# A linear-attention and gated-FFN kernel: ten gathering copies moved from SyncE's queue to GpSimd's, and per-tile waits for the pool of FFN weights

## The chip, the cores and the metric

The kernel runs on one core of one Trainium2 chip. The metric is the device time of one execution in microseconds (us); lower is better. The engines are TensorE (PE, with its weight loads PEld), VectorE (DVE), ScalarE (ACT), GpSimd (POOL) and SyncE (SP). Each engine works off its own row of instructions in order. Transfers are issued by an instruction on SP, ACT or POOL and then run by themselves.

## The reference

There are S = 2048 tokens of width D = 576, 32 heads of width 18, and an FFN of width F = 4608; all is float32.

```
xn = layernorm(x)
q, k, v = split(xn @ wqkv)                     # 32 heads of 18
pq, pk = q @ w_phi, k @ w_phi                  # a matrix of 18 x 18 for each head
phi_q = [softmax(pq), softmax(-pq)]            # 36 features a head
phi_k = [softmax(pk), softmax(-pk)]
num = phi_q @ (phi_k^T v);  den = phi_q . sum(phi_k) + 1e-6
s = (num / den) @ wo
g = silu((silu(xn @ w_gate) * (xn @ w_up)) @ w_down)
out = x + s * g
```

## The kernel before

Every float32 operand of a product is split into a high part and a rest, both fp32r (`split`, L62 to L64: a cast on ACT, a subtraction on DVE), and a product is three matmuls. The tokens are worked in tiles of 128.

**Stages.** First comes the layernorm. Then in the K/V stage each token tile gives its features `phi` (`k_tile`), and `kv_step` sums `phi^T v` in PSUM (`kvp`). Then the Q stage: for each token tile `q_tile` computes `e` (the softmax parts, L312 to L325), multiplies it with the sums of the keys into `ez` (L627), divides, and writes `e` (L637); `numer` transposes `e` on PE (L656) and multiplies with the numerator's weights; `project` multiplies with `wo` (L697). Last comes the FFN, in which gate and up products (L815) and down products (L936) are done by a scheme of seven products for eight, with sums of weights and operands made on POOL. Matmuls of some early FFN tiles (`early_weights`, `early_tile`, L97 for the matmuls) are put between those of the Q stage. The weights of such a tile are loaded into `raw` (L114, on SP), cast into `wh` (L67, ACT), and completed on DVE (L68, L69).

**The numerator's weights.** Behind the K/V stage `kvp` is masked into `km` (L561) and split. The groups of seven heads go to `KVH` and `KVL`. The last group, of four heads (72 rows), is split into `km2`, which lies in a buffer named `phi` of the pool `kk`. It is packed so that one matmul holds more rows: ten small transfers from SBUF to SBUF (four of 54 x 72 and six of 18 x 72 numbers) gather the parts into `KVP` (108 partitions). PE reads `KVP` at L669, with `et`, a packed copy of the last group of `e` that ACT makes (L641 and L642).

**Sums of the token blocks.** The FFN's scheme needs sums of blocks of tokens. For one block after another, POOL adds them (`raw_x`, `sums`), ACT and POOL split them (`sum_parts`, L364 to L366), and SP stores them to `sum_dram` (L367, L368). The last block is done at the beginning of the Q stage.

**What sets the order.** The engines' rows are set when the kernel is built: a scheduler takes the instructions as they are written, `tc.high_priority` moves some ahead where their inputs allow, and `tc.issue_after` holds some back. Waits between engines are set by the data, and by memory. A pool's tiles may take the place of tiles of a pool that is closed. With `reuse_waits="tile"` a new tile waits for those older tiles whose places it takes; without it the pool's first tile waits for all that lay in the memory that the pool takes over. The pool `fw` of the FFN's weights (L729) has no such argument: its tiles are `ld` (one loaded block of gate and up weights, L763), `ts` (sums of it), `w2` and `w1` (split parts, shown as `w`), and `wt`, which DVE clears once (L734). The Q stage's pool `qk` takes over memory of `kk`: its first `ez` has the place of `km2`.

**The opening of the FFN.** POOL makes four sums from `ld` (L791 to L794), ACT and DVE split `ld` and the sums (L63, L64), PE multiplies into `px`, `py`, `pw` (L815), and ACT copies `px` to `py` (L869) and to `s` (L844). POOL's `td` (L1058) is a sum of down weights that were loaded into `acc` (L1182). On POOL's row the stores of the last early tile (L137) stand between these sums.

Of the kernel before, what the change touches and what calls it, by code (L numbers as in the profile page):

```python
# [9 lines left out]
F32 = mybir.dt.float32  # L10
# [7 lines left out]
S, D, H, DH, F = 2048, 576, 32, 18, 4608  # L18
P = 128
# [10 lines left out]
NL = GROUPS[-1][1]  # L30
NK = NL + NL // 2
N3 = NK // 2
# [10 lines left out]
def heads(ap):  # L43
    return ap.rearrange("p (h d) -> p h d", d=DH)


def spread(ap, n):
    return ap.unsqueeze(2).to_broadcast([P, n, DH])
# [3 lines left out]
def gated_hedgehog_kernel(ctx: ExitStack, tc, x, w_qk, w_v, w_phi, wo, w_gu, w_tail, w_down, ident_in, mask_in, out):  # L52
# [5 lines left out]
    nc = tc.nc  # L58
# [3 lines left out]
    def split(hi, lo, src):  # L62
        nc.scalar.copy(hi, src)  # L63
        nc.vector.tensor_sub(lo, src, hi)  # L64
# [19 lines left out]
    def block(t):  # L84
        return t // HT, (t % HT) // 4, slice((t % 4) * P, (t % 4 + 1) * P)

    def xw(ps, i, j, cols, wh, wl, stationary_x):
        pairs = []
        for k in range(2):
            b = XB[i][2 * j + k]  # L90
            for c in range(2):
                pairs += [(b[:, c, cols], w[:, k, c]) for w in (wh, wl)]
                pairs += [(b[:, 3 + c, cols], wh[:, k, c])]
            pairs += [(b[:, 2, cols], wh[:, k, 2])]
        for n, (a, b) in enumerate(pairs):
            l, r = (a, b) if stationary_x else (b, a)
            last = nc.tensor.matmul(ps, l, r, start=n == 0, stop=n == len(pairs) - 1)  # L97
        return last
# [42 lines left out]
    with ExitStack() as att:  # L141
# [17 lines left out]
        with ExitStack() as wst:  # L159
# [191 lines left out]
            def sums(k):  # L351
                r = raws[k]
                nc.gpsimd.tensor_add(r[:, 3], r[:, 2], r[:, 3])
                nc.gpsimd.tensor_sub(r[:, 2], r[:, 0], r[:, 2])
                nc.gpsimd.tensor_sub(r[:, 0], r[:, 3], r[:, 0])
                nc.gpsimd.tensor_sub(r[:, 1], r[:, 1], r[:, 0])

            def sum_parts(k):
                r = raws[k]
                lo = los[k] = kk.tile([P, 4, 2, P], F32R, name="slo", bufs=1)  # L360
                for a in (2, 0):
                    j = slice(a, a + 2)
                    hi = his[k, a] = kk.tile([P, 2, 3, P], F32R, name="shi", bufs=2)
                    tc.keep_in_program_order(nc.scalar.copy(hi, r[:, j]))  # L364
                    nc.gpsimd.tensor_sub(hi[32:64, :, 2], r[32:64, j, 2], hi[32:64, :, 2])
                    nc.gpsimd.tensor_sub(lo[:, j], r[:, j, 0:2], hi[:, :, 0:2])  # L366
                    nc.sync.dma_start(sum_dram[k // 4, :, j, k % 4, 0:3], hi.bitcast(F32))  # L367
                    nc.sync.dma_start(sum_dram[k // 4, :, j, k % 4, 3:5], lo[:, j].bitcast(F32))  # L368
# [162 lines left out]
        with ExitStack():  # L531
            qc = att.enter_context(tc.tile_pool(name="qc", bufs=1, reuse_waits="tile"))
            KVH = qc.tile([GW, 2 * NG - 2, GW], F32R, name="KVH")
            KVL = qc.tile([GW, 2 * NG - 2, GW], F32R, name="KVL")
            zb = qc.tile([P, 2 * D], F32, name="zb")
            zc = qc.tile([GW, 12], F32, name="zc")
            m4 = mask.rearrange("p h d -> p (h d)")
            km2 = kk.tile([P, 2 * D], F32R, name="phi", bufs=2)[0:NL, 0:4 * NL].rearrange("p (a s n) -> p a s n", a=2, s=2)
            km2 = [km2[:, a] for a in range(2)]
            banks = [(i, 4 if i < 2 else 2, GROUPS[2 * i][1]) for i in range(3)]  # L540
            for i, n, w in banks:
                nc.scalar.copy(zc[0:w, 4 * i:4 * i + n], kvp[i][0:w, 0:n, w])
            z2, oz = zb.rearrange("p (s n) -> p s n", s=2), GROUPS[-1][0]

            def z_rows(d, g, s):
                w = GROUPS[g][1]
                nc.tensor.matmul(d, zc[0:w, 2 * g + s:2 * g + s + 1].to_broadcast([w, P]), ident[0:w, 0:w],
                                 start=True, stop=True)

            for s, name in enumerate(("vx", "vy")):  # L550
                zp = kps.tile([P, 512], F32, name=name)
                for g, (o, w) in enumerate(GROUPS[:-1]):
                    z_rows(zp[:, o:o + w], g, s)
                nc.scalar.copy(z2[:, s, 0:oz], zp[:, 0:oz])
            zp = kps.tile([P, 512], F32, name="vx")
            for s in range(2):
                z_rows(zp[:, s * NL:(s + 1) * NL], NG - 1, s)
            nc.scalar.copy(z2[:, :, oz:D], zp[:, 0:2 * NL].rearrange("p (s n) -> p s n", s=2))
            for i, n, w in banks:
                km = qc.tile([GW, 4, GW], F32, name="km")  # L560
                nc.vector.tensor_mul(km[0:w, 0:n, 0:w], kvp[i][0:w, 0:n, 0:w],  # L561
                                     m4[0:w, 0:w].unsqueeze(1).to_broadcast([w, n, w]))
                kh, kl = (t[0:w, 4 * i:4 * i + n, 0:w] for t in (KVH, KVL)) if n == 4 else km2
                split(kh, kl, km[0:w, 0:n, 0:w])
            KVP = qc.tile([NK, 3, NL], F32R, name="KVP")
            for s in range(2):
                for a, t in enumerate(km2):
                    nc.sync.dma_start(KVP[s * N3:(s + 1) * N3, a].bitcast(F32), t[0:N3, s].bitcast(F32))
                for b, t in enumerate((km2[0], *km2)):
                    r = (2 * b + s) * DH  # L570
                    nc.sync.dma_start(KVP[r:r + DH, 2].bitcast(F32), t[N3:NL, s].bitcast(F32))

        raw_x(order[7], 0, 1)
        raw_x(order[7], 2, 3)
        sums(order[7])
        sum_parts(order[7])
        kst.close()
        eps = est.enter_context(tc.tile_pool(name="eps2", bufs=2, space=PSUM, reuse_waits="tile"))
        with ExitStack() as qst:
# [38 lines left out]
            def q_tile(t):  # L618
                i0, j0, cols = block(t)
                pq = qps.tile([P, 2, 512], F32, name="p2")  # L620
                for i in range(2):
                    w = slice(i * HALF, (i + 1) * HALF)
                    xw(pq[:, i, 0:HALF], i0, j0, cols, QH[:, :, :, w], QL[:, :, :, w], True)
                e = qk.tile([P, 2 * D], F32, name="e", bufs=4)
                r = softmax_parts(pq, e).rearrange("p (s h) -> p s h", s=2)
                ez = qk.tile([P, 2 * D], F32, name="ez", bufs=1)
                nc.vector.tensor_mul(ez, e, zb)  # L627
                y = qk.tile([P, 2 * H], F32, name="y")
                nc.vector.reduce_sum(y, heads(ez), axis=AX.X)
                y2 = y.rearrange("p (s h) -> p s h", s=2)  # L630
                nc.vector.scalar_tensor_tensor(y2[:, 0], r[:, 0], DEN_EPS, y2[:, 0], op0=ALU.mult, op1=ALU.add)
                nc.vector.tensor_mul(y2, y2, r[:, ::-1])
                den = qk.tile([P, H], F32, name="den")
                nc.vector.tensor_add(den, y2[:, 0], y2[:, 1])
                nc.vector.reciprocal(den, den)
                nc.vector.tensor_mul(y2, r[:, ::-1], den.unsqueeze(1).to_broadcast([P, 2, H]))
                last_e.append(nc.vector.tensor_mul(heads(e), heads(e), spread(y, 2 * H)))  # L637
                et = qk.tile([P, 2, NK], F32, name="et", bufs=2)
                o = GROUPS[-1][0]
                e2 = e.rearrange("p (s n) -> p s n", s=2)  # L640
                nc.scalar.copy(et[:, 0].rearrange("p (s n) -> p s n", s=2), e2[:, :, o:o + N3])  # L641
                nc.scalar.copy(et[:, 1].rearrange("p (b s n) -> p b s n", b=3, s=2),  # L642
                               e2[:, :, o + N3:D].unsqueeze(1).to_broadcast([P, 3, 2, DH]))
                return e, et

            def numer(es):
# [61 lines left out]
            for n in range(S // QS + 1):  # L708
                new = []
                if n > 0:  # L710
                    om = numer(es)
                if n < S // QS:
                    new += [q_tile(order[n] * (QS // P) + j) for j in range(QS // P)]
                if n == 0:
                    split_wo()
                if n > 0:
                    project(order[n - 1], *om, n == S // QS)
                es = new
# [7 lines left out]
            for i in halves:  # L726
                early_tile(f, i, parts, (1,) if f == 1 else (0, 1), behind=read[2 * NT + 1] if f == 1 else None)

    fw = ctx.enter_context(tc.tile_pool(name="fw", bufs=1))  # L729
    fp = ctx.enter_context(tc.tile_pool(name="fp", bufs=1, reuse_waits="tile"))  # L730
    acc = fp.tile([P, 4, HT // 2, HALF], F32, name="acc")
    wts = [fw.tile([P, 7, P], F32R, name=f"wt{k}") for k in range(2)]
# [531 lines left out]
```

## Time and profile before

| | before |
|---|---|
| median of 3 runs | 1598.11 us (1595.94, 1598.11, 1599.13) |
| the profiled execution, its own time | 1597.25 us |
| its span in the trace | 1595.4 us |
| granted TensorE clock in it | 0.998 of full speed |
| PE busy | 1575.6 us, 99% |
| DVE busy | 1166.3 us, 73% |
| ACT busy | 732.6 us, 46% |
| POOL busy | 663.1 us, 42% |

The span runs from the first to the last instruction in the trace; the time of the execution has 1.85 us more around it. A busy share is that of the whole span. The times of single instructions below are microseconds from the start of the span.

### The profile page before, as it was taken

How to read it: one execution, taken by the hardware profiler on the slowest of the kernel's cores; microseconds unless marked ns; L12 is line 12 of the kernel's file. 1: busy time of each engine (PE TensorE's matmuls, PEld its weight loads, DVE VectorE, ACT ScalarE, POOL GpSimd, SP SyncE). 2: the span in 40 equal slices, each digit the busy share in tenths (PEclk: the TensorE clock that was granted, in tenths of full speed). 3: DMA queues.
4: the chain of work that ended last, by engine and by line, in shares of the span. 5: the costliest groups of instructions: out<-in, count | busy, mean ns of one | idle time of the engine just before them, and what ended most of it. 6: DMA issues, size and time to landing. Idle time of an engine off the chain costs nothing.

```text
span 1595.4 us, 25391 instructions
## 1 busy us (share of the span) xinstructions
PE 1575.6 (99%) x9367; PEld 1415.4 (89%) x9367; DVE 1166.3 (73%) x1737; ACT 732.6 (46%) x1437; POOL 663.1 (42%) x714
## 2 busy tenths in 40 slices
PE   9999999999999999999999999999999999999998
PEld 6899997999987888988888888888888888888887
DVE  7777768999956778987777778645667667666577
ACT  5633335554435654445444444454343343333334
POOL 3676751434115635644535445223324324133133
PEclk9999999999999999999999999999999999999999
DMA  9522234446438454455545453874545664556435
GB/s 306 198 82 80 101 113 142 130 113 195 137 136 279 164 185 166 169 188 178 179 160 206 159 203 116 323 230 143 162 138 146 184 194 160 170 182 188 143 118 179
DMA packets 124460, 269.14 MB, mean 169 GB/s; under 512 B 13608, under 2 KB 55272, under 8 KB 123056
## 3 DMA queue, kind: packets, MB, share of 16 engines
q1 hardware_dynamic: 108890, 245.58, 46.8%
q0 software_dynamic: 3552, 12.59, 2.8%
q10 hardware_dynamic: 11894, 9.35, 1.8%
q8 instruction: 74, 1.21, 0.3%
q14 instruction: 50, 0.41, 0.1%
HBM read 167.53 MB, written 99.09 MB: 167 GB/s over the span
## 4 chain that ended last, share of the span: by engine, by line
PE 93%; DMA 2%; DVE 2%; POOL 1%; issue 1%; ACT 1%; SPq 1%; POOLq 0%; ACTq 0%; DVEq 0%
PE px L815 25%; PE pd L936 24%; PE pw L815 12%; PE p L97 7%; PE py L815 6%; PE pe L97 4%; PE p L697 4%; PE kvp L333 2%; PE pt L669 2%; PE vx L421 1%; PE pt L656 1%; PE vw L421 1%; PE tp L252 1%; DMA h_dram<-h 1%; PE vx L97 1%
## 5 line engine op out<-in xcount | busy, mean ns | idle before, releaser
L936 PEld LDWEIGHTS pd<-dw,hh 128*128 128x128 f32 x3012 | 424.7, 189 | 22.0 <-ACT pd L991 1.5
L936 PE MATMUL pd<-dw,hh 128*128 128x288 f32 x3012 | 438.7, 295 | 1.6 <-ACT pd L991 0.7
L815 PE MATMUL px<-X,w 128*128 128x512 f32 x1512 | 386.3, 390 | 4.1 <-ACT s L844 3.0
L815 PEld LDWEIGHTS px<-X,w 128*128 128x128 f32 x1512 | 274.5, 188 | 51.5 <-ACT s L844 3.7
L815 PE MATMUL pw<-X,w 128*128 128x512 f32 x744 | 188.8, 389 | 0.0
L815 PEld LDWEIGHTS pw<-X,w 128*128 128x128 f32 x744 | 139.6, 188 | 28.9
L1098 DVE TENSOR_TENSOR acc<-pd,acc 128x576 f32<-128x576 f32 x128 | 96.3, 753 | 94.1 <-PE pd L936 93.5
L849 DVE TENSOR_TENSOR s<-pw,s 128x512 f32<-128x512 f32 x126 | 86.5, 687 | 90.5 <-ACT s L844 80.2
L844 ACT COPY s<-px 128x512 f32<-128x512 f32 x126 | 73.8, 586 | 146.0 <-PE px L815 145.9
L63 ACT CAST hh<-ha 128x512 fp32r<-128x512 f32 x140 | 82.8, 619 | 94.2 <-PE pd L936 68.7
L64 DVE TENSOR_TENSOR hh<-ha,hh 128x512 fp32r<-128x512 f32 x140 | 109.5, 808 | 18.8 <-ACT hh L63 18.6
L1070 POOL TENSOR_TENSOR hb<-hb 128x512 f32<-128x512 f32 x34 | 45.9, 1350 | 158.8 <-DVE hb L861 155.7
L97 PE MATMUL pe<-X,wh 128*128 128x512 f32 x340 | 107.1, 397 | 0.0
L64 DVE TENSOR_TENSOR w<-ld,w 128x512 fp32r<-128x512 f32 (+1 forms) x96 | 77.8, 812 | 37.6 <-ACT w L63 36.9
L815 PE MATMUL px<-X,wt 128*128 128x512 f32 x252 | 98.3, 390 | 0.0
L815 PE MATMUL py<-X,w 128*128 128x512 f32 x378 | 96.5, 390 | 0.0
L1083 POOL TENSOR_TENSOR ha<-ha 128x512 f32<-128x512 f32 x34 | 52.6, 1562 | 100.4 <-DVE hh L64 100.4
L791 POOL TENSOR_TENSOR ts<-ld 128x256 f32<-128x256 f32 x32 | 27.8, 867 | 152.1 <-issue 69.7
L1057 POOL TENSOR_TENSOR h<-ha,hb 128x512 f32<-128x512 f32 x34 | 45.0, 1323 | 108.8 <-DVE ha L865 76.4
L63 ACT CAST w<-ld 128x512 fp32r<-128x512 f32 (+1 forms) x96 | 52.7, 549 | 80.0 <-POOL ld L794 46.9
L869 ACT COPY py<-px 128x512 f32<-128x512 f32 x63 | 36.1, 573 | 103.6 <-PE px L815 87.7
L815 PEld LDWEIGHTS py<-X,w 128*128 128x128 f32 x378 | 68.3, 188 | 10.7
(306 smaller groups left out, 3232.8 us busy)
## 6 DMA issues: line engine op xcount, KB each, us to landing
w_dram<-w SPq DMA_DIRECT2D x90, 512.0 KB
w<-w_dram SPq DMA_DIRECT2D x90, 512.0 KB
wt<-t_dram SPq DMA_DIRECT2D x62, 336.0 KB
ld<-in_B_w_gu SPq DMA_DIRECT2D x32, 512.0 KB
rt<-in_B_w_down SPq DMA_DIRECT2D x33, 288.0 KB
rb<-in_B_w_down SPq DMA_DIRECT2D x33, 288.0 KB
w_dram<-w SPq DMA_DIRECT2D x30, 256.0 KB
w<-w_dram SPq DMA_DIRECT2D x30, 256.0 KB
```

The lines of the kernel that those rows point to most:

```text
L63: nc.scalar.copy(hi, src)
L64: nc.vector.tensor_sub(lo, src, hi)
L97: last = nc.tensor.matmul(ps, l, r, start=n == 0, stop=n == len(pairs) - 1)
L697: nc.tensor.matmul(ps[:, 0:HALF], a, bw, start=k == 0, stop=k == len(mm) - 1)
L815: nc.tensor.matmul(ps, l, r, start=first and n == 0, stop=last and n == len(mm) - 1, skip_group_check=True)
L844: snaps.append(nc.scalar.copy(t, ps))
L849: nc.vector.tensor_add(t, ps, t)
L936: nc.tensor.matmul(ps, l, r, start=first and n == 0 and m == 0, stop=n == len(hs) - 1 and m == 2, skip_group_check=True)
L1057: sub(s, g["h"][0][0], g["h"][0][1])
L1070: nc.gpsimd.tensor_add(a21, a21, g["h"][1][1])
L1083: sub(a12, a12, g["h"][0][0])
L1098: nc.vector.tensor_add(a2, pd[:, :, 0:HALF], a2)
```

## The change

The ten transfers into `KVP` are issued by POOL in place of SP, and stand in the program behind the last block's sums. ACT's two copies into `et` are written under `tc.high_priority()`. The pool `fw` gets `reuse_waits="tile"`. No computation changes.

```diff
--- before.py
+++ after.py
@@ -563,17 +563,17 @@
                 kh, kl = (t[0:w, 4 * i:4 * i + n, 0:w] for t in (KVH, KVL)) if n == 4 else km2
                 split(kh, kl, km[0:w, 0:n, 0:w])
             KVP = qc.tile([NK, 3, NL], F32R, name="KVP")
-            for s in range(2):
-                for a, t in enumerate(km2):
-                    nc.sync.dma_start(KVP[s * N3:(s + 1) * N3, a].bitcast(F32), t[0:N3, s].bitcast(F32))
-                for b, t in enumerate((km2[0], *km2)):
-                    r = (2 * b + s) * DH
-                    nc.sync.dma_start(KVP[r:r + DH, 2].bitcast(F32), t[N3:NL, s].bitcast(F32))
 
         raw_x(order[7], 0, 1)
         raw_x(order[7], 2, 3)
         sums(order[7])
         sum_parts(order[7])
+        for s in range(2):
+            for a, t in enumerate(km2):
+                nc.gpsimd.dma_start(KVP[s * N3:(s + 1) * N3, a].bitcast(F32), t[0:N3, s].bitcast(F32))
+            for b, t in enumerate((km2[0], *km2)):
+                r = (2 * b + s) * DH
+                nc.gpsimd.dma_start(KVP[r:r + DH, 2].bitcast(F32), t[N3:NL, s].bitcast(F32))
         kst.close()
         eps = est.enter_context(tc.tile_pool(name="eps2", bufs=2, space=PSUM, reuse_waits="tile"))
         with ExitStack() as qst:
@@ -638,9 +638,10 @@
                 et = qk.tile([P, 2, NK], F32, name="et", bufs=2)
                 o = GROUPS[-1][0]
                 e2 = e.rearrange("p (s n) -> p s n", s=2)
-                nc.scalar.copy(et[:, 0].rearrange("p (s n) -> p s n", s=2), e2[:, :, o:o + N3])
-                nc.scalar.copy(et[:, 1].rearrange("p (b s n) -> p b s n", b=3, s=2),
-                               e2[:, :, o + N3:D].unsqueeze(1).to_broadcast([P, 3, 2, DH]))
+                with tc.high_priority():
+                    nc.scalar.copy(et[:, 0].rearrange("p (s n) -> p s n", s=2), e2[:, :, o:o + N3])
+                    nc.scalar.copy(et[:, 1].rearrange("p (b s n) -> p b s n", b=3, s=2),
+                                   e2[:, :, o + N3:D].unsqueeze(1).to_broadcast([P, 3, 2, DH]))
                 return e, et
 
             def numer(es):
@@ -726,7 +727,7 @@
             for i in halves:
                 early_tile(f, i, parts, (1,) if f == 1 else (0, 1), behind=read[2 * NT + 1] if f == 1 else None)
 
-    fw = ctx.enter_context(tc.tile_pool(name="fw", bufs=1))
+    fw = ctx.enter_context(tc.tile_pool(name="fw", bufs=1, reuse_waits="tile"))
     fp = ctx.enter_context(tc.tile_pool(name="fp", bufs=1, reuse_waits="tile"))
     acc = fp.tile([P, 4, HT // 2, HALF], F32, name="acc")
     wts = [fw.tile([P, 7, P], F32R, name=f"wt{k}") for k in range(2)]
```

How the change moves instructions is seen in the rows of the engines, as they stand in the built program. Behind the change lines are numbered anew (L568 becomes L573, L763 becomes L764).

On SP, at the end of the K/V stage, this is the difference (- before, + after; `h_dram` takes early FFN tiles, `sraw` is a block of tokens that is loaded for the sums):

```order
 L344 DMA sraw<-x_dram 128x4x128
 L137 DMA h_dram<-h 128x512
-L568 DMA KVP<-phi 54x72 x2
-L571 DMA KVP<-phi 18x72 x3
-L568 DMA KVP<-phi 54x72 x2
-L571 DMA KVP<-phi 18x72 x3
 L367 DMA sum_dram<-shi 128x2x384
 L368 DMA sum_dram<-slo 128x2x256
```

Ten transfers are gone from ahead of the stores of the last block's sums, and nothing takes their place. On POOL the same place reads, before (`tl` are sums of the FFN's weight tails, later stored to `t_dram`, L614):

```order
L354 TENSOR_TENSOR sraw<-sraw 128x384
L355 TENSOR_TENSOR sraw<-sraw 128x384
L356 TENSOR_TENSOR sraw<-sraw 128x384
L365 TENSOR_TENSOR shi<-sraw,shi 32x2x128
L366 TENSOR_TENSOR slo<-sraw,shi 128x512
L365 TENSOR_TENSOR shi<-sraw,shi 32x2x128
L366 TENSOR_TENSOR slo<-sraw,shi 128x512
L605 TENSOR_TENSOR tl<-tl 128x128
L606 TENSOR_TENSOR tl<-tl 128x128
```

and after:

```order
L356 TENSOR_TENSOR sraw<-sraw 128x384
L573 DMA KVP<-phi 54x72 x2
L365 TENSOR_TENSOR shi<-sraw,shi 32x2x128
L366 TENSOR_TENSOR slo<-sraw,shi 128x512
L365 TENSOR_TENSOR shi<-sraw,shi 32x2x128
L366 TENSOR_TENSOR slo<-sraw,shi 128x512
L576 DMA KVP<-phi 18x72 x3
L573 DMA KVP<-phi 54x72 x2
L576 DMA KVP<-phi 18x72 x3
L605 TENSOR_TENSOR tl<-tl 128x128
```

Two transfers stand ahead of the split of the sums and eight behind it. DVE's first `ez` (L627), whose place is that of `km2`, waits in both kernels for all ten transfers.

On SP, at the end of the Q stage, with what each waits for in brackets (DMAHW are transfers issued by SP or ACT, PE and Activation the engines), before:

```order
L677 DMA km<-lo 36x256 [waits DMAHW1_49,DMAHW0_49,DVE_49]
L677 DMA km<-lo 36x256
L763 DMA ld<-in_B_w_gu 128x4x256 [waits DMAHW1_49,DMAHW0_49,DMAHW5_49,PE_49,Activation_49]
L763 DMA ld<-in_B_w_gu 128x4x256 [waits DMAHW7_49]
L1182 DMA acc<-in_B_w_down 128x576 x2
```

and after:

```order
L678 DMA km<-lo 36x256 [waits DMAHW7_49,DMAHW6_49,DVE_49]
L678 DMA km<-lo 36x256
L764 DMA ld<-in_B_w_gu 128x4x256 [waits DMAHW3_49]
L764 DMA ld<-in_B_w_gu 128x4x256 [waits DMAHW5_49]
L1183 DMA acc<-in_B_w_down 128x576 [waits DMAHW6_49,PE_49]
L1183 DMA acc<-in_B_w_down 128x576 [waits DMAHW7_49]
```

The order is the same. The first `ld` waited for PE (the last matmul of L697) and ACT, and now does not; the wait for PE stands at the load of `acc` behind it. The rows of PE, DVE and ACT stand in the same order in both kernels, the copies into `et` among them.

## Rows read from the trace of the kernel before

**Rows 1.** The page: span, and busy time of each engine.

```profile
span 1595.4 us, 25391 instructions
...
PE 1575.6 (99%) x9367; PEld 1415.4 (89%) x9367; DVE 1166.3 (73%) x1737; ACT 732.6 (46%) x1437; POOL 663.1 (42%) x714
```

**Rows 2.** PE's waits: who waited for whom; us in total, times, longest.

```profile
PE px L815 <- ACT s L844: 3.0, 2, 2.5
...
PE pt L656 <- ACT et L641: 2.1, 1, 2.1
PE p L97 <- DVE e L317: 1.7, 1, 1.7
...
PE px L815 <- ACT py L869: 0.9, 1, 0.9
...
PE px L815 <- ACT h L132: 0.2, 1, 0.2
```

**Rows 3.** The chain that ended last, 215 to 290 us: start, length, what.

```profile
231.66 0.70 SPq L571
...
240.92 6.48 DMA raw<-in_B_w_gu
...
262.37 0.66 PE pt L656 x6
```

**Rows 4.** Timeline of SP: start, length, engine, line, operation, [idle before <- releaser].

```profile
234.07 0.67 SPq L368 DMA_DIRECT2D sum_dram<-slo  x1
```

**Rows 5.** Timeline of POOL, the last block's sums.

```profile
225.97 0.73 POOL L365 TENSOR_TENSOR shi<-sraw,shi 32x256 fp32r<-32x256 f32 x1
...
228.97 1.29 POOL L366 TENSOR_TENSOR slo<-sraw,shi 128x512 fp32r<-128x512 f32 x1
```

**Rows 6.** Timeline of DVE, the first tiles of the Q stage.

```profile
231.63 0.69 DVE L136 TENSOR_TENSOR h<-pe,h 128x512 f32<-128x512 f32 x1 [3.42 <-PE pe L97]
...
235.59 1.35 DVE L627 TENSOR_TENSOR ez<-e,zb 128x1152 f32<-128x1152 f32 x1
...
240.62 0.76 DVE L317 TENSOR_TENSOR e<-p,m 128x576 f32<-128x576 f32 x1
...
247.53 0.83 DVE L68 TENSOR_TENSOR wl<-raw,wh 128x512 fp32r<-128x512 f32 x1 [1.74 <-ACT wh L67]
...
260.70 1.35 DVE L637 TENSOR_TENSOR e<-e,y 128x1152 f32<-128x1152 f32 x1
```

**Rows 7.** Timeline of ACT, the cast ahead of the copies into `et`.

```profile
246.66 0.83 ACT L67 CAST wh<-raw 128x768 fp32r<-128x768 f32 x1 [2.26 <-DMA raw<-in_B_w_gu]
```

**Rows 8.** Issues by tile or line: ns min/median/max, first and last start; landing of `t_dram`.

```profile
L614 POOL DMA_DIRECT2D t_dram<-th x64: 496/497/515, 265.5 to 410.3; - x64
...
DMA to landing us min/median/max: 2.1/2.8/6.1
...
L571 SPq DMA_DIRECT2D KVP<-phi x6: 697/698/704, 226.4 to 231.7; - x6
...
L137 SPq DMA_DIRECT2D h_dram<-h x12: 325/355/952, 218.4 to 449.9; - x12
```

**Rows 9.** Timeline of SP, end of the Q stage.

```profile
452.57 1.52 SPq L677 DMA_DIRECT2D km<-lo  x2
465.61 1.30 SPq L763 DMA_DIRECT2D ld<-in_B_w_gu  x2
```

**Rows 10.** Timeline of ACT, opening of the FFN.

```profile
470.61 0.62 ACT L63 CAST w<-ld 128x512 fp32r<-128x512 f32 x1 [4.64 <-DMA ld<-in_B_w_gu]
...
478.58 0.40 ACT L63 CAST w<-ld 128x256 fp32r<-128x256 f32 x1 [3.07 <-POOL ld L794]
...
481.98 0.43 ACT L63 CAST dw<-td 128x288 fp32r<-128x288 f32 x1 [2.15 <-POOL td L1058]
...
508.70 0.41 ACT L63 CAST w<-ld 128x256 fp32r<-128x256 f32 x1 [3.73 <-POOL ld L794]
```

**Rows 11.** Timeline of PE, opening of the FFN.

```profile
511.71 1.70 PE L815 MATMUL px<-X,w 128*128 128x512 f32 x6 [2.53 <-ACT s L844]
```

## The prediction

> **What bounds the kernel now.** I read the page first. TensorE (PE) is busy for 1575.6 of 1595.4 us [rows 1], so this change can win only by ending PE's waits, and lose only by adding some. The list of PE's waits is therefore the second view [rows 2]. Two of its rows touch the copies into `KVP`: 2.1 us for `et` (L641), and 1.7 us for DVE's `e` (L317). Three rows belong to the opening of the FFN: 0.9 us for `py` (L869), 0.2 us for `h` (L132), and two waits of 3.0 us in all for `s` (L844), the longer of 2.5 us. These five rows hold 7.9 us.
>
> The chain that ended last tells what stands behind the first [rows 3]. SP, the queue that starts most transfers, is occupied by the ten `KVP` issues until 231.66 + 0.70 = 232.36. Then come the stores of the last sum block, the last of which starts at 234.07 [rows 4], the loads of `wo` and the load of an early FFN weight, `raw`, whose transfer ends at 240.92 + 6.48 = 247.40. ACT stood idle 2.26 us for it, then cast it (L67), and only behind that cast stand the two copies into `et` [rows 7]. The wait for `e` has another cause: DVE works without a pause from 231.63, when PE's early tile lets it go on, up to that `e` at 240.62 [rows 6]. It is no matter of queues.
>
> For the opening I read SP and ACT. SP is done with the Q stage at 452.57 + 1.52 = 454.09, yet starts the first `ld` at 465.61 [rows 9], because the pool `fw` takes over memory of pools of the Q stage, and by its rule the first tile waits for all of them, the last projection matmul (L697) among them. ACT idles 4.64 us for this `ld`, later 3.07 us for POOL's sum from `ld` and 2.15 us for POOL's `td` [rows 10].
>
> **Part B, `et` at high priority.** The row orders of PE, DVE and ACT are the same before and after, so `et` still stands behind the cast. It costs and gives nothing.
>
> **Part A, first effect: SP.** SP loses ten issues. The sum stores now wait for POOL's sums alone. These ended at 228.97 + 1.29 = 230.26 [rows 5]; two `KVP` issues now stand ahead of them on POOL, each c us long, so the sums end at 230.26 + 2c. With c = 0.50 (below) that is 231.26, and the last store can start at about 231.3, since the others go out as their halves are done. It started at 234.07, so all of SP's later loads move up by about 2.8 us. `raw` needs 2.26 us to be there when ACT comes to it [rows 7]. So `et` is in time, and PE's 2.1 us end. Not all of it is kept. DVE waited only 1.74 us for the same cast (L68, 247.53), and it is what PE meets next: its product `e` (L637) ended at 260.70 + 1.35 = 262.05 [rows 6], and PE's transposes of it began at 262.37 [rows 3]. PE cannot come forward there by more than DVE does. I take **1.8 us**; the bounds are 1.7 and 2.1.
>
> **Part A, second effect: the copies land later.** This price decides the case. DVE's first `ez` (L627) lies in the memory of the packed weights, and the order shows that it waits for all ten copies. It started at 235.59, and DVE had no pause before it [rows 6], so a later landing stops DVE, then its `e`, then PE, us for us: DVE works without a pause up to that `e`, for which PE waits already [rows 2].
>
> POOL issues two copies at 225.97 and eight behind the sums. The last issue starts at 230.26 + 2c + 7c; it lands l later. The stall is
>
> X = 230.26 + 9c + l − 235.59 = 9c + l − 5.33.
>
> The trace has no such copy on POOL. The nearest rows are its stores to `t_dram`: c = 0.497, and l from 2.1 through 2.8 to 6.1 us [rows 8]. With c = 0.50 and l = 2.8 X is 1.97, and I take **2.0 us**, since these are the same queue and the same engine with comparable numbers of rows (32 against 18 or 54). With l = 2.1 X is 1.3. With l = 6.1, the longest, X is 5.3; I give that end little weight, since the copies carry at most 54 rows of 288 bytes, where a store carries 32 of 3.5 KB. With SP's own price, c = 0.698 [rows 8], X is 3.75. On SP a `KVP` copy costs about twice an `h_dram` store (0.698 against 0.355 [rows 8]); were that ratio of 1.97 to hold on POOL, c would be 0.98 and X 6.3. At the lower end the copies could be issued while POOL's sums run, or land much sooner, and X is 0. On POOL itself little waits behind: its next rows are the sums of `tl`, which are wanted by the stores to `t_dram` from 265.5 on [rows 8], and the issues would end at about 235.3. PE's own reading of `KVP` comes behind the transposes of 262.37 [rows 3].
>
> The Trainium skill, page "DMA: Bandwidth & Descriptors", section "Anatomy of one DMA — SWDGE (gpsimd) path", gives such a transfer a fixed cost of about 2.0 us plus its bytes at 436 GB/s. By that the small copies would land 2.0 us after issue, X would be 1.2 and the time 0.8 us lower; the trace's shortest landing, 2.1 us, is close to it, and its median of 2.8 us is not.
>
> **Part C, the pool's waits tile by tile.** In the order after, the first two `ld` loads no longer wait for PE or ACT; each waits for one earlier transfer. They can start when SP is free, at about 454. Issued at 465.61, the first was cast at 470.61 [rows 9, 10], 5.0 us later; issued at 454 to 455 it lands before 461. ACT's first cast can follow its last work of the Q stage at about 466, 4.6 us sooner [rows 10]. POOL's first sum follows, but its second stands behind an `h_dram` store on POOL's queue that waits for PE's early tile, so of the 4.6 us some 2.3 come through to the sums that ACT waits for. Its cast at 478.58 then comes at about 476.3, the one at 481.98 at 479.5 or before. PE lost 0.9 us behind the first, 0.5 us (3.0 − 2.5) behind the second and 0.2 us ahead of both [rows 2]. All are shorter than the advance. I take the full **1.6 us**; the lower bound is 0, if PE's waits there should turn out to have another cause close behind. The wait of 2.5 us at 511.71 [rows 11] I leave as it is: ACT's cast ahead of it waits 3.73 us for POOL [rows 10], whose sums follow tiles that move with PE.
>
> **Sum.** 2.0 − 1.8 − 1.6 = −1.4 us. On the profiled execution, 1597.25 us, that is 1595.85. This execution lies 0.86 us below the median of the runs, 1598.11; from the median the forecast is **1596.7 us**. The runs of before spread from 1595.94 to 1599.13, which is 0.2%. I take 0.2%, 3.2 us, as what a measurement can tell: faster is below 1594.9, slower above 1601.3.
>
> **Rivals.**
> First, the other side: POOL pays for a copy inside the chip what SP pays, twice its price of a store. For it speaks SP's ratio in [rows 8]; against it, that the two queues make their transfers differently, and POOL's price hardly varies (0.496 to 0.515). Then X = 6.3 and the sum is +2.9: 1601.0 us. The change loses from X above 3.4, that is c above 0.66 at l = 2.8; it is slower beyond the measurement from X above 6.6. A stretched issue on POOL would do the same by another way: at c = 0.9 X is 5.6, the sum +2.2 and the time 1600.3 us. The Trainium skill, in the same page's section "SWDGE vs HWDGE vs iDMA", says that DVE can lock GpSimd out of the memory in which it writes its descriptors; the trace does not bear this out, since 64 stores, issued while DVE was three quarters busy, differ by 0.02 us. I give the two together 0.16, of which 0.03 is for the stretched issue.
>
> Second, the copies are hidden (X = 0): they land before DVE comes to `ez`. Then the sum is −3.4, and 1594.7 us; with the whole 2.1 us of `et`, 1594.4. For it speaks that such small copies may land in less than 2.1 us, or be issued faster; against it, that nine issues of 0.50 us leave them only 0.83 us to land in. 0.10.
>
> Third, the gain of the opening is given back: PE comes 1.6 us earlier to 511.71, but the sums of POOL don't, and the wait there grows from 2.5 to 4.1. The sum is +0.2, and 1598.3 us. For it speaks ACT's wait for POOL of 3.73 us [rows 10]; against it, that POOL's work there starts behind DVE and PE. 0.14.
>
> My own forecast has 0.60. **Range:** 1594.0 to 1601.0. It takes in the hidden copies below, with some scatter of the runs, and above X up to 6.3; what is left out is the upper half of the first rival and the far tails. Faster: two thirds of the second rival and a small part of my own, 0.12. Slower: half of the first rival, and 0.01 of the rest, 0.09. Same: 0.79.
>
> **What the profile after would show.** The price c is in POOL's rows of `KVP` (0.50 each), l in their landing. X is DVE's idle time before the first `ez`, put down to `KVP`: 2.0 us, and PE's wait for `e` grows from 1.7 to 3.7. PE's wait for `et` is gone, or under 0.4. The last `sum_dram` store starts at about 231.3. The first `ld` is issued before 456, and the waits for `py`, `h` and the shorter `s` are gone, while the one of 2.5 us stays. I would be wrong if POOL's issue took 0.7 us or more, if the copies landed after 238.5, or if the wait at 511.71 grew.

## The result, and the profile after

The changed kernel takes 1600.43 us (median of 16 runs, 1597.88 to 1603.77), the kernel before 1596.62 us beside it (16 runs). The ratio is 1.0023, with an interval of 1.0015 to 1.0030: slower by 3.7 us, between 2.4 and 4.8. I had forecast 1.4 us less than before. The median lies inside the range that I gave; its sign is not the forecast one. The profiled execution took 1601.42 us.

The page of the kernel after, span and busy times:

```profile
span 1599.6 us, 25391 instructions
...
PE 1577.0 (99%) x9367; PEld 1418.0 (89%) x9367; DVE 1171.9 (73%) x1737; ACT 732.5 (46%) x1437; POOL 668.7 (42%) x724
```

The span grew by 4.2 us, PE's busy time by 1.4. So most of the loss is waiting, and some is PE working more slowly. PE's waits after (us in total, times, longest):

```profile
PE p L97 <- DVE e L317: 7.7, 1, 7.7
PE px L816 <- ACT s L845: 2.9, 2, 2.5
```

The waits of [rows 2] for `et`, `py` and `h` are gone, as forecast. The shorter wait for `s` should have gone too, but it stayed: 0.4 us for 0.5 before. But the wait for DVE's `e` grew from 1.7 to 7.7 us, which decides the result. One instruction of DVE's timeline tells what it waited for:

```profile
241.02 1.43 DVE L627 TENSOR_TENSOR ez<-e,zb 128x1152 f32<-128x1152 f32 x1 [5.59 <-DMA KVP<-phi]
```

In [rows 6] this `ez` started at 235.59 without a pause. X, which I had put at 2.0, is 5.59. The tile `KVP` splits it into price of issue and landing (ns min/median/max, first and last start; landing in us):

```profile
L576 POOL DMA_DIRECT2D KVP<-phi x6: 505/506/510, 231.0 to 234.5; - x6
L573 POOL DMA_DIRECT2D KVP<-phi x4: 523/535/548, 225.6 to 233.0; - x4
...
  DVE ez L627: 5.6, 1
...
DMA to landing us min/median/max: 1.6/5.1/6.5
```

The issue costs 0.51 to 0.54 us, as taken (0.50), and the last one starts at 234.5, close to the formula (230.26 + 9 × 0.50 = 234.8). The landing is what was missed. The chain that ended last has it (start, length, what):

```profile
234.50 6.21 DMA KVP<-phi
```

The last copy took 6.2 us from issue to landing; the shortest took 1.6 us, the median is 5.1. SP's timeline shows what else was started then:

```profile
231.05 0.36 SPq L368 DMA_DIRECT2D sum_dram<-slo  x1
231.50 0.87 SPq L588 DMA_DIRECT2D oh<-in_A_wo  x2
...
233.76 1.24 SPq L603 DMA_DIRECT2D tl<-in_B_w_tail  x2
...
235.61 17.20 SPq L114 DMA_DIRECT2D raw<-in_B_w_gu  x3
```

The last sum store starts at 231.05 (forecast 231.3; [rows 4] had 234.07), and the loads follow at once. POOL's last eight copies were issued from 230.96 to 235.0, in the middle of these. How busy the DMA engines were stands in the last column but one of the following rows, first after, then before (columns: stretch, us, busy us and count of PE, PEld, DVE, ACT, POOL, granted clock, DMA share, GB/s):

```profile
232.00:234.00 2.00, 2.00 (x18) 2.00 (x16) 1.99 (x5) 0.05 (x1) 2.00 (x4) 1.00 0.95 231
```

```profile
228.00:230.00 2.00, 2.00 (x10) 1.66 (x9) 0.21 (x1) 1.59 (x3) 1.84 (x3) 1.00 0.03 5
```

In both stretches copies into `KVP` are being issued, after at a DMA share of 0.95, before at 0.03. It was not DVE that held the copies up: from 235.43 until `ez` it stood idle, while the last of them were still on their way. That the loads delay the copies is so far a reading; the experiments test it.

The granted clock is the second loss. Two stretches of the kernel after, then one of the kernel before, in which PE does the same product (columns as above):

```profile
243.00:246.00 3.00, 0.00 (x0) 0.00 (x0) 3.00 (x6) 0.60 (x1) 2.36 (x6) 0.50 0.01 3
252.00:253.00 1.00, 1.00 (x6) 1.00 (x6) 0.97 (x2) 1.00 (x2) 0.00 (x0) 0.50 0.09 16
```

```profile
242.00:243.00 1.00, 1.00 (x10) 1.00 (x9) 1.00 (x1) 0.98 (x2) 0.00 (x0) 1.00 1.04 287
```

While PE idled, the clock fell to 0.50, which is 1.2 GHz, and it was still there when PE worked again: six matmuls in a microsecond where the kernel before did ten. The first and the last row of that product on PE, after and before:

```profile
247.28 0.58 PE L97 MATMUL p<-QH,X 128*128 128x288 f32 x1 [7.73 <-DVE e L317]
...
253.58 0.43 PE L97 MATMUL p<-QH,X 128*128 128x288 f32 x2
```

```profile
241.52 0.37 PE L97 MATMUL p<-QH,X 128*128 128x288 f32 x1 [1.73 <-DVE e L317]
...
245.17 0.42 PE L97 MATMUL p<-QH,X 128*128 128x288 f32 x2
```

Between them lie 6.30 us after and 3.65 before. The early tile behind the product starts 6.06 us later than before, where 5.76 of the pause less 2.13 of the wait for `et` would make 3.6; so the clock cost some 2.5 us. Nor is this execution alone in it: over the 16 runs of the changed kernel the mean granted clock is 0.994 to 0.998, over the runs of the kernel before in the experiments 0.997 to 1.000.

The rest went about as forecast. ACT casts `wh` without waiting for `raw` ([rows 7] had 2.26 us), and at the opening of the FFN the first `ld` is issued as soon as SP is free. From the timelines of ACT and SP after:

```profile
249.89 0.81 ACT L67 CAST wh<-raw 128x768 fp32r<-128x768 f32 x1
...
472.23 0.62 ACT L63 CAST w<-ld 128x512 fp32r<-128x512 f32 x1 [0.41 <-ACT e L704]
...
482.56 0.41 ACT L63 CAST w<-ld 128x256 fp32r<-128x256 f32 x1 [3.07 <-POOL ld L795]
```

```profile
460.06 1.30 SPq L764 DMA_DIRECT2D ld<-in_B_w_gu  x2
```

PE comes to the opening 5.9 us later than before (its last early tile ends there). Measured against that, ACT's first cast came 4.3 us sooner (472.23, for 470.61 + 5.9) and the one behind POOL's sums 1.9 us sooner (482.56, for 478.58 + 5.9); I had expected 4.6 and 2.3. On PE:

```profile
487.44 1.65 PE L816 MATMUL px<-X,w 128*128 128x512 f32 x6 [0.37 <-ACT s L845]
...
516.26 2.08 PE L816 MATMUL px<-X,w 128*128 128x512 f32 x4 [2.53 <-ACT s L845]
```

The wait of 2.53 us is as long as in [rows 11], and it starts 4.55 us later than before. The opening thus gave back about 1.3 us of the 5.9.

### The profile page after: what moved, and what is told of

It is laid out like the page before. It is cut to its first block, busy times and chain, and to the rows that moved or that the text cites. A ratio compares the mean times of both kernels' runs of the same rounds, so it can differ in the third digit from the quotient of the medians.

```text
span 1599.6 us, 25391 instructions
## 1 busy us (share of the span) xinstructions
PE 1577.0 (99%) x9367; PEld 1418.0 (89%) x9367; DVE 1171.9 (73%) x1737; ACT 732.5 (46%) x1437; POOL 668.7 (42%) x724
## 4 chain that ended last, share of the span: by engine, by line
PE 91%; DMA 3%; POOL 2%; DVE 2%; issue 1%; ACT 1%; SPq 0%; ACTq 0%; POOLq 0%; DVEq 0%
PE px L816 24%; PE pd L937 24%; PE pw L816 12%; PE p L97 7%; PE py L816 6%; PE pe L97 4%; PE p L698 4%; PE kvp L333 2%; PE pt L670 2%; PE vx L421 1%; PE pt L657 1%; PE vw L421 1%; PE tp L252 1%; DMA h_dram<-h 1%; DMA raw<-in_B_w_gu 0%
```

## The experiments

The theory was: the copies land late because the same change lets SP's loads start ahead of them, and all share the DMA engines; DVE's `ez` waits for the landing; PE idles and its clock falls. The first rival was that a copy issued by POOL lands late whatever else moves. The second was that the FFN pool brought the loss. Each time is a median beside runs of the kernel before on the same chip.

### The two parts alone: c_alone and a_alone

c_alone is the kernel before with one edit, and a_alone the changed kernel without it:

```diff
-    fw = ctx.enter_context(tc.tile_pool(name="fw", bufs=1))
+    fw = ctx.enter_context(tc.tile_pool(name="fw", bufs=1, reuse_waits="tile"))
```

> Only the pool of FFN weights waits tile by tile; the copies into KVP stay on SP. Theory (the whole loss lies in the copies, the opening gains): the first ld is issued near 454 us, PE's waits for py and h go, and the kernel is 1.2 to 1.9 us faster than before. Rival (the earlier ld loads collide with something in the opening and give back what they win): within 0.5 us of before. If the pool's change caused the loss, it is 2 us or more slower.

> Only the copies into KVP are issued by POOL behind the last sums (with et at high priority); the FFN pool as before. Theory: DVE waits about 5.6 us for the copies, PE idles near 7.7 us, its granted clock falls to half behind that, and the kernel is about 6 us slower than before. Rival (the loss of the changed kernel comes mostly from the pool of FFN weights): under 2 us slower.

c_alone took 1594.40 us against 1596.48, ratio 0.9985 (0.9977 to 0.9994), 1 to 4 us faster. a_alone took 1602.94, ratio 1.0040 (1.0026 to 1.0054), 6.4 us slower. By these ratios the two parts make +6.4 and −2.4 us, together +4.0, which is close to the +3.7 of the whole change. PE's waits of a_alone:

```profile
PE p L97 <- DVE e L317: 7.5, 1, 7.5
...
PE px L816 <- ACT py L870: 0.9, 1, 0.9
```

The long wait for `e` belongs to the move of the copies; the wait for `py`, which the whole change ended, is back without the pool's part. The rival that the pool lost is out; the copies are the whole loss. In c_alone the first `ld` is issued at 455.05, and the waits for `py` and `h` are gone, 1.1 us in all.

### The copies ahead of the sums: pool_first

```diff
-        sum_parts(order[7])
         for s in range(2):
             for a, t in enumerate(km2):
...
+        sum_parts(order[7])
```

> The changed kernel, but all ten copies stand on POOL ahead of the split of the last sums, so that SP's stores and loads start behind them. Theory (the copies land late because the stores and loads of SP fill the DMA engines): each lands within about 2 us, the last near 233, DVE has no pause ahead of ez; the sum stores start some 4 us later than in the changed kernel, so the wait for et is as before or about 1 us longer; with the gain of the FFN opening the kernel is 0 to 2 us faster than before. Rival (a transfer issued by POOL between such small pieces of memory lands 5 us or more after issue whatever else moves): the last lands near 236, DVE still waits 0.5 us or more.

It took 1595.47 us, ratio 0.9994 (0.9984 to 1.0004): as fast as before. Issue and landing of `KVP` in it:

```profile
L575 POOL DMA_DIRECT2D KVP<-phi x6: 507/508/520, 225.6 to 229.2; - x6
...
DMA to landing us min/median/max: 1.6/1.6/1.7
```

The same ten copies, issued by the same engine at the same price, land in 1.6 us when SP's stores and loads start behind them. The rival expected 5 us or more and falls. DVE has no pause ahead of `ez`, as expected. What I had not expected is that PE still waited 3.7 us for `e`, and then not for `et`:

```profile
PE p L97 <- DVE e L317: 3.7, 1, 3.7
```

DVE's timeline and POOL's show why:

```profile
230.73 2.81 DVE L68 TENSOR_TENSOR wl<-raw,wh 128x512 fp32r<-128x512 f32 x2
233.56 1.76 DVE L69 TENSOR_TENSOR wh<-raw,wh 32x256 fp32r<-32x256 f32 x2
```

```profile
231.92 1.07 POOL L365 TENSOR_TENSOR shi<-sraw,shi 32x256 fp32r<-32x256 f32 x1
233.07 1.63 POOL L366 TENSOR_TENSOR slo<-sraw,shi 128x512 fp32r<-128x512 f32 x1
```

POOL's last subtractions now run beside DVE's, and both are stretched: L68 and L69 take 2.81 and 1.76 us for 1.28 and 0.75 before, L366 takes 1.63 for the 1.29 of [rows 5]. That makes 2.5 us on DVE's path. That running side by side is what stretches them is a reading; it was not tried apart.

### Only SP's loads held back: sp_holds and sp_holds_all

Here POOL's row is that of the changed kernel. A small transfer on SP reads `KVP`, so that the loads behind it on SP wait for the copies. sp_holds read one plane of three, sp_holds_all reads all:

```diff
+    mark = dram.tile([NK, 3, 8], F32, name="mark")
...
+            nc.sync.dma_start(mark, KVP[:, :, 0:8].bitcast(F32))
             for g, (o, w) in enumerate(GROUPS):
                 nc.sync.dma_start(wrs[g // 2][0:w, g % 2], wo[o:o + w, :])
```

> The changed kernel, with one small added transfer on SP (108 x 8 numbers out of KVP into a scratch tensor) ahead of the loads of wo, so that SP starts those loads, tl and raw only when all ten copies have landed; POOL's row and the sum stores are as in the changed kernel. Theory (the loads that SP brings forward fill the DMA engines ahead of the copies): the last copies land within 1.6 to 2.5 us of issue, DVE waits 0.5 to 1.5 us for them in place of 5.6, and the loads start near 237; the wait for et comes back, 3 to 4 us long, as raw is some 2 us later than before. In all within 1 us of before, about 3 us faster than the changed kernel. Rival (copies issued by POOL behind its sums land 5 us or more after issue anyway): DVE waits 5 us again, and the kernel is slower than the changed one.

> As sp_holds, but the small transfer on SP reads all three planes of KVP, so that SP's loads wait for all ten copies; in sp_holds it read the first plane alone, and the loads started at 233.9, ahead of the last copies' landing. Theory (the loads delay the copies): the longest landing is 2 us or less, against 3.6 in sp_holds and 6.5 in the changed kernel; DVE waits 0.3 to 1.2 us; the loads start near 236.5, and PE waits 2 to 4 us for et. In all -1 to +1.5 us against before. Rival (the copies behind POOL's sums are slow by themselves, and the marker helped by chance): longest landing 3 us or more.

sp_holds took 1597.49 us, ratio 1.0011 (1.0002 to 1.0020), 1.8 us slower than before where I had expected at most 1. Landing of `KVP`, then SP's timeline, then DVE's:

```profile
DMA to landing us min/median/max: 1.6/1.7/3.6
```

```profile
233.46 0.32 SPq L588 DMA_DIRECT2D mark<-KVP  x1
233.88 0.77 SPq L590 DMA_DIRECT2D oh<-in_A_wo  x2
```

```profile
237.73 1.36 DVE L629 TENSOR_TENSOR ez<-e,zb 128x1152 f32<-128x1152 f32 x1 [3.00 <-DMA KVP<-phi]
```

My bound of 1.5 us for DVE's wait was missed too: with one plane read, the loads went out at 233.88, when POOL was still issuing, and the last copies were caught again. sp_holds_all mends that. It took 1597.37 us, ratio 1.0002 (0.9992 to 1.0012). The same views, with PE's waits and, last, the stretch in which most copies land:

```profile
DMA to landing us min/median/max: 1.5/1.6/2.4
```

```profile
237.48 0.94 SPq L588 DMA_DIRECT2D mark<-KVP  x1
238.53 0.93 SPq L590 DMA_DIRECT2D oh<-in_A_wo  x2
```

```profile
237.52 1.36 DVE L629 TENSOR_TENSOR ez<-e,zb 128x1152 f32<-128x1152 f32 x1 [1.19 <-DMA KVP<-phi]
```

```profile
PE p L98 <- DVE e L318: 3.0, 1, 3.0
...
PE pt L659 <- ACT et L644: 2.8, 1, 2.8
```

```profile
234.00:236.00 2.00, 2.00 (x18) 2.00 (x17) 1.96 (x4) 0.00 (x0) 2.00 (x5) 1.00 0.10 24
```

The DMA share there is 0.10, where the changed kernel had 0.95. The longest landing of 2.4 us misses my bound of 2 and lies below the 3 of the rival; the loads start at 238.53, where I had expected 236.5. With nothing changed but the small transfer and the moment at which SP's loads start, the longest landing went from 6.5 through 3.6 to 2.4 us, and DVE's wait from 5.6 through 3.0 to 1.2. That shows from the other side that the loads, and not POOL's place behind the sums, make the copies late. The price is the wait for `et`, which is back with 2.8 us: the loads are late again.

### The copies land late and nobody waits: own_place, own_sp, own_late

Two tiles that are needed late (`ph`, `pl`) are given the place of the packed weights, ahead of `ez`. own_place is the changed kernel with this; own_sp has the copies on SP as before, with the same place and the pool's change; own_late has all ten on POOL behind the sums.

```diff
+                if not last_e:
+                    for name in ("ph", "pl"):
+                        qk.tile([GW, 2, QS], F32R, name=name, bufs=2)
                 ez = qk.tile([P, 2 * D], F32, name="ez", bufs=1)
```

> The changed kernel, but two late tiles of the Q stage take the place of the packed weights, so that DVE's first ez no longer waits for the ten copies; these run as in the changed kernel. Theory (the landing costs time only through that wait): DVE has no pause ahead of ez, PE's wait for e is 1.7 us again, the clock stays at full speed, the wait for et is gone, and the kernel is 3 to 4 us faster than before, 7 to 8 us faster than the changed one. Rival (POOL's transfers slow DVE, SP or the other transfers by themselves, or the next user of KVP stalls instead): less than 1.5 us faster than before.

> The copies stay on SP as before; the packed weights have their place under two late tiles, and the pool of FFN weights waits tile by tile. It differs from the run own_place only in the queue of the copies, so the two together give the price of the move without its landing. Theory (moving the copies off SP is worth the wait for et, 1.8 to 2.1 us, when nothing waits for their landing): the wait for et is here, about 2 us, and the kernel is about as fast as c_alone, 1.5 to 2.2 us slower than own_place. Rival (place alone, or the pool, made own_place fast): within 0.8 us of own_place.

> As own_place, but all ten copies stand on POOL behind the last sums (two stood ahead). The sum stores and the loads of SP start about 1.1 us sooner. Theory (in own_place nothing waits for these any more, PE's wait for et being gone): within 0.6 us of own_place, 3 to 4.5 us faster than before. Rival (the copies ahead of the sums still cost): 1 us faster than own_place.

own_place took 1592.60 us, ratio 0.9976 (0.9967 to 0.9984). Landing of `KVP`, DVE's `ez`, and ACT's cast of `wh`:

```profile
DMA to landing us min/median/max: 1.6/4.3/6.1
```

```profile
235.73 1.35 DVE L630 TENSOR_TENSOR ez<-e,zb 128x1152 f32<-128x1152 f32 x1
```

```profile
244.45 0.82 ACT L67 CAST wh<-raw 128x768 fp32r<-128x768 f32 x1
```

The copies land almost as late as in the changed kernel, and it costs nothing: DVE has no pause, PE waits 1.7 us for `e` as before, and not for `et`. It is 7.5 us faster than the changed kernel when each is taken against its own runs of before (7.8 by medians), and only the place of a tile was changed. So the late landing costs only by DVE's wait for a place in memory.

own_sp took 1594.99 us, ratio 0.9990 (0.9981 to 0.9999), and waits for `et`:

```profile
PE pt L659 <- ACT et L644: 1.4, 1, 1.4
```

It is 2.2 us slower than own_place by the ratios (2.4 by medians), and like c_alone: this is what the move itself is worth once its landing is hidden; 1.8 had been forecast. The size is rough, since the runs scatter by 3 to 4 us, and only 1.4 us of it are the wait for `et`; the rest was not followed up. own_late took 1592.59 us, ratio 0.9977 (0.9968 to 0.9986), the same as own_place, although its copies, which are issued sooner, take longer still from issue to landing:

```profile
DMA to landing us min/median/max: 2.6/6.0/6.8
```

Both beat the kernel before by 3 to 4 us and the changed one by 7 to 8.

## Why the prediction was wrong

**The step that failed** is the landing in "the copies land later". I had both ends, 2.1 and 6.1 us, and took 2.8, "since these are the same queue and the same engine"; I gave the long end little weight because the copies are small. The last copy took 6.2 us and was there at 240.71, past the 238.5 that I had named as a sign of being wrong. Size was the wrong argument. The shortest landing shows what a small copy needs, 1.6 us; the rest is the load on the DMA engines, which in the kernel after were at a share of 0.85 to 1.06 from 230 to 242 (stretches of 2 us). The load was no accident either. It was the gain that I had counted one paragraph earlier: SP's loads 2.8 us sooner. The two effects of part A were costed apart, and one is the cause of the other. The Trainium skill, page "DMA: Bandwidth & Descriptors", section "Issuing engines are not separate DMA queues", states that transfers started by different engines run on the same DMA engines and interleave, and that starting them from several engines saves only the time to issue. sp_holds_all and pool_first agree that they share these engines: with SP's loads held back the median landing is 1.6 us, against 5.1.

**The step that was missing** is the clock. I let PE lose "us for us" what DVE waits. PE lost 2.5 us more, since the product behind the pause ran at half the clock for most of its length.

**By terms**, forecast and read in the trace: X 2.0 and 5.6, which became 6.0 in PE's wait, as DVE's operations behind it took 0.3 us longer and PE came to the wait 0.2 us earlier; the clock 0 and 2.5; the wait for `et` −1.8 and −2.1; the opening −1.6 and −1.3. The sum read is 5.1, less the 0.2 us by which PE was early. The span grew by 4.2; the other 0.7 us are small differences elsewhere that were not followed up.

**What was right.** The price c (0.50, read as 0.51 to 0.54), and with it the case against the first rival: POOL does not pay SP's double price. The formula for X holds with the measured landing: the last copy was there at 234.50 + 6.21 = 240.71, DVE had been free since 241.02 − 5.59 = 235.43, and 0.3 us passed from the landing to DVE's start; 5.28 + 0.31 is 5.59. Part B did nothing: the order is the same. The opening's gain is there in c_alone alone as well: 2.1 us by medians, between 1 and 4, of which the trace shows the 1.1 us of waits that went; 1.6 had been forecast. The wait at 511.71 stayed at 2.5 us in c_alone too, so the third rival is out. One reading was too low: the stores to `t_dram` were issued while DVE was busy for 94% of the time (265 to 411 us), not three quarters, so that argument is stronger than it was put.

**The rivals.** The second one, hidden copies, was wrong for this kernel. Its sum, without a wait of DVE, describes own_place: 1594.4 was its time for such a kernel, and with the medians of before at 1596.5 instead of 1598.1, 3.7 us below is 1592.8; 1592.6 was measured. The first rival gave 1601.0 for X = 6.3. The time came out near that, through another mechanism: the landing, not the issue. That 1600.43 lies inside the range is luck as well: the sum had no clock in it, but it started from 1598.1, which is 1.5 us above the median of the 16 runs of before.

## What to carry to other kernels

A transfer taken out of a queue does not only leave a gap: what moves up into the gap competes with it. Cost a move between queues with the load that the engines will have after the move, not with a landing taken from a quiet or a different stretch. Before moving a transfer later, look for who waits for its source's memory, not only for its destination: here the reader of `KVP` had some 30 us to spare, and the next owner of the source's place had none. A stall of PE of some microseconds can cost more than its length; look at the granted clock behind it.

## What the runs showed of the hardware

- The same copies of 5 to 15 KB landed in 1.6 to 1.7 us (pool_first, all ten) and in up to 6.8 us (own_late), according to what else the DMA engines carried: a share of 0.06 while pool_first issued them (224 to 231), of 0.85 and more in own_late (230 to 234).
- A copy from one place of the on-chip memory to another costs POOL 0.51 to 0.54 us to issue, SP 0.70 [rows 8]; here POOL was the cheaper issuer.
- The granted clock fell to 0.50 behind PE's waits of 7.7 us (after), 7.5 (a_alone), 4.8 (sp_holds) and 3.7 (pool_first). It stayed at 1.00 behind waits of 3.0 and 2.8 us in sp_holds_all, and of 1.7 and 2.1 in the kernel before. But in c_alone's execution, with waits of 1.7 and 2.0 us at the same place, it fell:

```profile
248.00:249.00 1.00, 1.00 (x4) 0.81 (x3) 0.97 (x2) 1.00 (x2) 0.00 (x0) 0.50 0.06 16
```

  The length of the last wait alone does not decide it. What does stays open here.
- In pool_first DVE's subtractions took more than twice as long while POOL's ran beside them (2.81 us for 1.28, 1.76 for 0.75), POOL's last two up to 1.5 times as long (1.07 for 0.73, 1.63 for 1.29).
